# Expert units: second products behind their own first products, another product order, other buffer counts

## The chip, the cores and the metric

The kernel runs as one program on one core of a Trainium2 chip. The metric is the device time of one execution in microseconds (us). Engines are named as in the profile: PE (TensorE, matmuls; PEld are its weight loads), DVE (VectorE), ACT (ScalarE), POOL (GpSimd) and SP (SyncE, which issues the DMAs of weights). PSUM is the memory that matmuls write to, in banks of 128x512 float32; SBUF holds all else.

## The reference, cut to what matters

```python
x = attention(q, k, v, proj)            # 2 x 768 tokens, 8 heads of 64, bucket mask
x = rational_ffn(x, w_in, w_out, a, b)  # h = x @ w_in; g = P(h) / Q(h); x = g @ w_out
# experts: N = 1536 tokens, D = 512, E = 8, F = 1024
P = exp(x @ w_gate - max)
for _ in range(8):                      # Sinkhorn: rows, then columns
    P /= P.sum(1, keepdims=True) + 1e-9
    P /= P.sum(0, keepdims=True) + 1e-9
    P *= N / E
out = 0
for e in range(E):
    out += P[:, e:e+1] * (relu(x @ w1[e]) @ w2[e])
```

All of it is float32. The kernel splits each operand into a high and a low part in a rounded type (`fp32r`) and sums three products, high x high, high x low and low x high.

## The kernel before, in words

The program has three stages: attention (to about 287 us of the profiled execution), the dense layer (to 578 us) and the experts (to the end). The change touches the end of the dense layer and the experts.

**Units.** The expert stage works on 64 units. Unit u is a quarter q of an expert's hidden columns (256 of them; q runs over 8 experts x 4) and a batch b of 768 tokens, u = 2q + b. With 256 hidden columns, 512 inputs and 768 tokens the first layer is a product of 2x2 blocks, done with seven products in place of eight (`unit_b`, L546). Product m multiplies a sum of weight blocks (`ww`, a tile for two of them, built by POOL in `w_blocks`, L497) by a sum of token blocks (`xb`, built once for each batch in `x_blocks`, L463). One product is six matmuls of 384 columns into one of four PSUM banks (`product`, L529).

**From a product to a hidden block.** ACT copies product 1 to `m1`; DVE adds the others to running sums `u2` and `u3`, and four times writes a hidden block `c` (L559). ACT rounds relu(c) to `gh` (L554), and DVE computes the low part `gl` from `c` and `gh` (L555), both of them in SBUF. A pair (gh, gl) is for a half f of the hidden columns and a half g of the tokens.

**Second products.** `second_b(u, t)` (L588), t = 0 to 5, multiplies 128 tokens of a token half g = t // 3 by the expert's second weights `wb` (split by POOL in `w_second`, L518): six matmuls of 512 columns into one of three PSUM banks, hidden half f = 0 first, then 1. DVE adds the bank to `osum`, times the gate's weight (L610; L608 while expert 0 runs, and ACT copies for q = 0).

**Order.** The stage is recorded by hand, step by step, and each engine executes its own instructions in that order. Before, the main loop (L883) puts one second product of unit u - 1 behind each first product of unit u but the first, and steps of the gate between them. `ORDER` (L427) is the order of the products. POOL's blocks for q + 1 are recorded step by step along the units of q, into five weight tiles used in turn (L494), so POOL has to wait until PE is done with a tile. `w_second(q)` is recorded in the first step of unit 2q.

**Gate.** `gate_steps` (L624) computes logits (`lp`, 40 matmuls), transposes them (`lt`), then the maximum and eight Sinkhorn iterations, in which PE sums columns (`cp`) and DVE does the rest. It uses a single PSUM bank of its own (`sum_bank(3, ..)`).

Of the kernel before, what the change touches and what calls it, by code (L numbers as in the profile page):

```python
# [15 lines left out]
F32R = mybir.dt.float32r  # L16
# [19 lines left out]
def kernel(  # L36
# [18 lines left out]
    B, H, S, D = q.shape  # L55
# [368 lines left out]

    ORDER = (1, 6, 7, 4, 2, 5, 3)  # L427
    xb, wb_, ww = {}, {}, {}

    def tokens(half, b, g, a, z):  # L430
# [32 lines left out]
    def x_blocks(b):  # L463

        x_given(b, 1, 0, 0, pool_lo)
        if b == 0:
            x_given(b, 2, 1, 0, pool_lo)
        yield
        t1 = x_temp("t1")
        for a, z in pieces(b, 0, 1):  # L470
            dve.tensor_tensor(t1[:, :, a:z], tokens(0, b, 1, a, z), tokens(0, b, 0, a, z), ALU.subtract)
        t2 = x_temp("t2")
        for a, z in pieces(b, 1):
            dve.tensor_tensor(t2[:, :, a:z], tokens(1, b, 1, a, z), t1[:, :, a:z], ALU.subtract)
        yield
        x_sum(b, 6, t2, dve_lo)
        x_sum(b, 5, t1, pool_lo)
        yield
        t3 = x_temp("t3")
        for a, z in pieces(b, 1):  # L480
            dve.tensor_tensor(t3[:, :, a:z], tokens(1, b, 1, a, z), tokens(0, b, 1, a, z), ALU.subtract)
        x_sum(b, 7, t3, pool_lo)
        yield
        for a, z in pieces(b, 0):
            dve.tensor_tensor(t2[:, :, a:z], tokens(1, b, 0, a, z), t2[:, :, a:z], ALU.subtract)
        x_sum(b, 4, t2, dve_lo)
        yield
        if b:
            x_given(b, 2, 1, 0, pool_lo)
        x_given(b, 3, 1, 1, pool_lo)  # L490

    def w_pair(q, k):

        r = (q * 4 + k) % 5  # L494
        return wslots[0].tile([P, 2, 2, 2, P], F32R, tag=("wa0", "wa1", "wa2", "wa3", "wb0")[r], name="ww")

    def w_blocks(q, stemp):  # L497

# [19 lines left out]
    def w_second(q):  # L518

        r = raws[1, CB + q]  # L520
        for f in range(2):
            k = (2 * q + f) % 4
            t = (wslots[0] if k < 3 else late).tile([P, 2, 512], F32R, tag=f"wb{k + 1}" if k < 3 else "w", bufs=1,
                                                    name="wb")
            split(pool_hi, pool_lo, t[:, 0], t[:, 1], r[:, f])
            wb_[q, f] = t
        load_weights(1, CB + q + 2)

    def product(o, q, b, m):  # L529
        w, x = ww[q, m], xb[b, m]  # L530
# [6 lines left out]
    bhid = {}  # L537

    def hidden_b(u, f, g):
        bhid[u, f, g] = tuple(late.tile([P, GC], F32R, tag=t, bufs=8, name=t) for t in ("gh", "gl"))  # L540
        return bhid[u, f, g]

    def temp_b(name, bufs=1):
# [2 lines left out]
    def unit_b(u):  # L546

        q, b = divmod(u, B)
        m1, u2, u3 = temp_b("m1"), temp_b("u2"), temp_b("u3")
        low = []  # L550

        def high(f, g, c):
            gh, gl = hidden_b(u, f, g)
            act.activation(gh, c, AF.Relu)  # L554
            low.append(lambda: dve.scalar_tensor_tensor(gl, c, 0.0, gh.bitcast(F32), ALU.max, ALU.subtract))  # L555

        def add(x, o, f, g):
            c = temp_b("c", 3)
            dve.tensor_tensor(c, o, x, ALU.add)  # L559
            high(f, g, c)  # L560

        def prod(m):
            o = hidden_bank(next(turn) % 4, "prod")[:, 0:GC]
            product(o, q, b, m)
            return o

        act_copy(m1, prod(1))
        yield
        dve.tensor_tensor(u2, prod(6), m1, ALU.add)
        yield  # L570
        dve.tensor_tensor(u3, prod(7), u2, ALU.add)  # L571
        yield
        add(u3, prod(4), 1, 0)
        yield
        low.pop()()
        add(m1, prod(2), 0, 0)
        yield
        low.pop()()
        p5 = prod(5)
        add(u3, p5, 1, 1)  # L580
        dve.tensor_tensor(u2, p5, u2, ALU.add)
        yield
        low.pop()()
        add(u2, prod(3), 0, 1)
        yield
        low.pop()()

    def second_b(u, t):  # L588

        q, b = divmod(u, B)  # L590
        e, p = divmod(q, FP)
        g, i = divmod(t, 3)
        o = sum_bank(0, "accb")
        ts = slice(i * P, (i + 1) * P)
        for f in range(2):
            gh, gl = bhid[u, f, g]
            w = wb_[q, f]
            for m, (l, r) in enumerate(((gh, w[:, 0]), (gh, w[:, 1]), (gl, w[:, 0]))):
                pe.matmul(o, lhsT=l[:, ts], rhs=r, start=f == 0 and m == 0, stop=f == 1 and m == 2)  # L599
        n = b * 6 + t  # L600
        if q == 0 and t % 2 == 0:
            k = n // 2
            osum[k] = sums.tile([P, 2, 512], F32, tag=f"sum{k // 2}{k % 2}", name="osum")
        d = osum[n // 2][:, t % 2]
        if q == 0:
# [18 lines left out]
    def gate_steps():  # L624

        gp = const.tile([P, NT, E], F32, name="gp")
        for b in range(B):
            for g in range(2):

                blocks = ((1, 0), (2, 1)) if g == 0 else ((1, 0), (5, 0), (3, 1))  # L630
                lp = sum_bank(3, "lp")
                ops = [(w, xb[b, m][:, j, c], 2 * half + c) for m, half in blocks for c in range(2)
                       for w, j in ((wg2, 0), (wg2, 1))]
                for n, (w, x, c) in enumerate(ops):
                    pe.matmul(lp[0:2 * E, 0:GC], lhsT=w[:, c], rhs=x, start=n == 0, stop=n == len(ops) - 1)
                yield
                ls = temp_b("ls")[0:2 * E]
                act_copy(ls, lp[0:2 * E, 0:GC])
                yield
                lt = sum_bank(3, "lt")  # L640
                for j in range(3):
                    pe.transpose(lt[:, 2 * j * E:2 * (j + 1) * E], ls[:, j * P:(j + 1) * P], idf[0:2 * E, 0:2 * E])
                n = b * 6 + g * 3
                yield
                dve.tensor_reduce(gp[:, n:n + 3, :], lt[:, 0:6 * E].rearrange("p (t k e) -> p t e k", k=2, e=E),
                                  AX.X, ALU.add)
        m1 = const.tile([P, 2], F32, name="gm")
        dve.tensor_reduce(m1[:, 0:1], gp, AX.XY, ALU.max)
        ones = temp_b("ls")[:, 0:P]
# [10 lines left out]
        yield  # L660
        dve.tensor_scalar(m1[:, 1:2], mb[:, 0:1], -1.0, None, ALU.mult)
        act.activation(gp, gp, AF.Exp, bias=m1[:, 1:2])
        yield
        rsum = const.tile([P, NT], F32, name="rsum")
        csum = const.tile([P, E], F32, name="csum")
        for _ in range(8):
# [1 line left out]
            dve.tensor_scalar(rsum, rsum, 1e-9, None, ALU.add)  # L668
            dve.reciprocal(rsum, rsum)
            dve.tensor_tensor(gp, gp, rsum.unsqueeze(2).broadcast_to((P, NT, E)), ALU.mult)  # L670
            yield
            yield
            cp = sum_bank(3, "cp")
            pe.matmul(cp[:, 0:NT * E], lhsT=ones, rhs=gp.rearrange("p t e -> p (t e)"), start=True, stop=True)
# [132 lines left out]
    with tc.manual_schedule(engines={mybir.EngineType.PE, mybir.EngineType.Activation, mybir.EngineType.DVE,  # L807
# [3 lines left out]
        for s in range(NS + QF):  # L811
# [41 lines left out]
                go(xgen)  # L853
            acting = [new] if n < 0 else []

            if s == NS - QS + ALAG + 3:
                def stemp():
                    c = [conv.tile([P, 512], F32, tag="c", name="c").rearrange("p (k c f) -> p k c f", k=2, c=2)
                         for _ in range(2)]
                    return c[0][:, 0], c[0][:, 1], c[1][:, 0]  # L860
                ws = w_blocks(0, stemp)
            if ws is not None and s < NS:
                go(ws)
            if n == 0:
                x_stack.close()
                xs[0] = ffn_pool("x0", 1)
# [10 lines left out]
        def stemp():  # L877
            t = x_temp("st").rearrange("p c (f k) -> p (c f k)", k=P).rearrange("p (k c f) -> p k c f", k=3, c=2)
            return t[:, 0], t[:, 1], t[:, 2]

        gating = gate_steps()
        SECOND = {1: 0, 2: 1, 3: 2, 4: 3, 5: 4, 6: 5}
        for u in range(NB_ + 1):  # L883
            q, b = divmod(u, B)
            first = unit_b(u) if u < NB_ else None
            for k in range(len(ORDER)):
                if first:
                    go(first)
                if u and k in SECOND:
                    second_b(u - 1, SECOND[k])  # L890
                if u >= 1:
                    go(gating)
                if u == 0:
                    if k == 0:
                        xgen = x_blocks(1)
                    go(xgen)
                if u < NB_:
                    if b == 0 and k == 0:
                        w_second(q)
                        ws = w_blocks(q + 1, stemp) if q + 1 < E * FP else None  # L900
                    if ws is not None and (b == 1 and k < 4 or b == 0 and 2 <= k < 5):
                        go(ws)
            if first:
                go(first)
            if u in (FP * B, FP * B + 1):
                weight_b(u - FP * B)


# [28 lines left out]
```

## Time and profile before

| | |
|---|---|
| median of 3 runs | 1613.9 us (1613.78 to 1615.29) |
| the profiled execution | 1613.6 us, span 1611.8 us |
| PE busy | 1549.2 us (96%), 8071 matmuls |
| DVE / POOL / ACT busy | 1224.9 / 930.0 / 621.0 us |
| mean granted TensorE clock | 0.994 |

The span runs from the first to the last instruction; 1.8 us lie around it. Matmuls are pipelined: a matmul's own duration (337 ns for 384 columns) is longer than the distance from its start to the next one's start, so PE's pace is read from starts and not from durations. "Idle before" gives what an engine waited for just before a group of instructions.

### The profile page before, as it was taken

What the parts mean: (1) busy time and instruction counts of PE and PEld (TensorE: products, weight loads), DVE (VectorE), ACT (ScalarE), POOL (GpSimd) and SP (SyncE); (2) the same over time, 40 slices, a digit from 0 to 9 for tenths busy, and PEclk for the clock granted to TensorE, in tenths of its full rate; (3) what the DMA queues carried; (4) which work ended last, traced back from release to release, by engine and by line L of the source; (5) the groups of instructions that cost most, each with busy time, mean ns of one, the idle gap of its engine ahead of it and who ended that gap; (6) DMA issues with size and microseconds to landing.
All of it is one profiled execution on the core that took longest, in us unless ns stands there. A gap on an engine that the chain in (4) does not pass through costs nothing.

```text
span 1611.8 us, 22139 instructions
## 1 busy us (share of the span) xinstructions
PE 1549.2 (96%) x8071; PEld 1354.4 (84%) x8071; DVE 1224.9 (76%) x2116; ACT 621.0 (39%) x1167; POOL 930.0 (58%) x1165
## 2 busy tenths in 40 slices
PE   5989999899999979999999999999999999999999
PEld 4888888777666868898989899898989989898987
DVE  7989989788999983786667767666766766676675
ACT  4888788787767833111111111111111111111111
POOL 7788785677777874456455345445534544553450
PEclk9999999999999989999999999999999999999999
DMA  5323220011111000011011001101100110110002
GB/s 168 86 81 90 69 76 15 27 53 61 57 53 66 1 26 27 27 40 40 27 34 45 27 27 40 40 27 38 42 27 27 40 40 27 39 40 27 27 1 78
DMA packets 49404, 71.83 MB, mean 45 GB/s; under 512 B 4368, under 2 KB 35088, under 8 KB 49296
## 3 DMA queue, kind: packets, MB, share of 16 engines
q1 hardware_dynamic: 48432, 68.85, 13.8%
q8 instruction: 64, 1.05, 0.3%
q10 hardware_dynamic: 864, 1.57, 0.3%
q14 instruction: 44, 0.36, 0.1%
HBM read 59.79 MB, written 3.15 MB: 39 GB/s over the span
## 4 chain that ended last, share of the span: by engine, by line
PE 71%; DVE 16%; ACT 5%; POOL 4%; issue 4%; DMA 1%; SPq 0%; POOLq 0%; DVEq 0%
PE accb L599 33%; PE prod L534 28%; PE av L323 2%; PE pt L308 2%; DVE tq L382 2%; DVE tu L384 2%; DVE tr L383 2%; POOL e L294 2%; PE acca L405 2%; PE h L354 1%; DVE e L285 1%; DVE bits L182 1%; DVE bits L180 1%; DVE tu L376 1%; DVE ptl L109 1%
## 5 line engine op out<-in xcount | busy, mean ns | idle before, releaser
L534 PE MATMUL prod<-xb,ww 128*128 128x384 f32 x2688 | 534.2, 337 | 5.7 <-DVE u L571 2.4
L534 PEld LDWEIGHTS prod<-xb,ww 128*128 128x128 f32 x2688 | 479.9, 189 | 40.7 <-ACT xb L106 2.9
L599 PE MATMUL accb<-wb,gh 128*128 128x512 f32 x1536 | 478.8, 393 | 0.0
L554 ACT ACTIVATE gh<-c 128x384 fp32r<-128x384 f32 x256 | 134.6, 526 | 764.5 <-DVE c L559 764.5
L610 DVE SCALAR_TENSOR_TENSOR osum<-accb,gp,osum 128x512 f32<-128x512 f32 x336 | 251.9, 750 | 208.3 <-PE accb L599 206.2
L599 PEld LDWEIGHTS accb<-wb,gh 128*128 128x128 f32 x1536 | 283.9, 188 | 36.4
L599 PE MATMUL accb<-wb,gl 128*128 128x512 f32 x768 | 305.9, 398 | 4.2 <-DVE gl L555 4.2
L100 POOL TENSOR_SCALAR ww<-ra 128x256 fp32r<-128x256 f32 x128 | 52.4, 410 | 407.9 <-PE prod L534 407.6
L555 DVE SCALAR_TENSOR_TENSOR gl<-c,gh 128x384 fp32r<-128x384 f32 x256 | 199.4, 779 | 4.5 <-ACT gh L554 4.3
L599 PEld LDWEIGHTS accb<-wb,gl 128*128 128x128 f32 x768 | 144.4, 188 | 35.1 <-DVE gl L555 4.6
L354 PE MATMUL h<-xh,wa 128*128 128x512 f32 x384 | 127.5, 395 | 5.8 <-DVE tu L377 5.6
L405 PE MATMUL acca<-gh,wb 128*128 128x512 f32 x384 | 128.0, 394 | 4.9 <-DVE part L417 2.6
L559 DVE TENSOR_TENSOR c<-prod,u 128x384 f32<-128x384 f32 x192 | 106.1, 552 | 27.2 <-PE prod L534 27.0
L109 DVE TENSOR_TENSOR ptl<-pt,pth 128x512 fp32r<-128x512 f32 x144 | 94.4, 681 | 19.0 <-ACT pth L106 18.2
L103 POOL TENSOR_TENSOR ww<-ra,ww 128x256 fp32r<-128x256 f32 x128 | 94.8, 740 | 10.7
L294 POOL TENSOR_SCALAR e<-e,rs 128x768 f32<-128x768 f32 x96 | 88.7, 934 | 19.6 <-DVE rs L292 10.1
L354 PEld LDWEIGHTS h<-xh,wa 128*128 128x128 f32 x384 | 72.1, 188 | 27.1 <-DVE tu L377 10.0
L405 PEld LDWEIGHTS acca<-gh,wb 128*128 128x128 f32 x384 | 72.1, 188 | 25.7 <-ACT gh L106 5.1
L285 DVE TENSOR_SCALAR_CACHE_REDUCE e<-s 128x768 f32<-128x768 f32 x96 | 90.8, 947 | 1.3 <-PE s L278 0.9
L308 PE MATMUL pt<-idr,e 128*128 128x128 f32 x576 | 81.3, 275 | 11.0 <-POOL e L294 4.7
L286 ACT ACTIVATE e<-e,nm 128x768 f32<-128x768 f32 x96 | 89.8, 935 | 3.5 <-DVE e L285 2.8
L103 POOL TENSOR_TENSOR wb<-rb,wb 128x512 fp32r<-128x512 f32 x64 | 84.3, 1317 | 5.3
(168 smaller groups left out, 2429.9 us busy)
## 6 DMA issues: line engine op xcount, KB each, us to landing
ra<-in_moe_w_dram SPq DMA_DIRECT2D x32, 512.0 KB
rb<-in_moe_w_dram SPq DMA_DIRECT2D x32, 512.0 KB
ra<-in_moe_w_in_dram SPq DMA_DIRECT2D x16, 512.0 KB
rb<-in_moe_w_out_dram SPq DMA_DIRECT2D x16, 512.0 KB
qkv<-in_q_dram SPq DMA_DIRECT2D x16, 192.0 KB
qkv<-in_k_dram SPq DMA_DIRECT2D x16, 192.0 KB
qkv<-in_v_dram SPq DMA_DIRECT2D x16, 192.0 KB
a<-a SPq DMA_DIRECT2D x16, 192.0 KB
```

Of the source, the lines that this page charges most:

```text
L103: pool.tensor_tensor(lo, src, hi.bitcast(F32), ALU.subtract)
L109: dve.tensor_tensor(lo, src, hi.bitcast(F32), ALU.subtract)
L285: dve.tensor_scalar(e[j], s[:, 0:S], BIG, None, ALU.min, ALU.min, accum_out=nm)
L294: pool.tensor_scalar(e[j], e[j], rs[:, j:j + 1], 0.0, ALU.mult, ALU.add)
L308: pe.transpose(pt[:, c, j * P:(j + 1) * P], e[j][:, cc * P:(cc + 1) * P], idf)
L354: pe.matmul(hps, lhsT=a[:, c], rhs=x[:, c], start=m == 0, stop=m == 3 * KC - 1)
L405: pe.matmul(o, lhsT=l[:, js], rhs=r, start=f == 0 and m == 0, stop=f == QF - 1 and m == 2)
L534: pe.matmul(o, lhsT=w[:, i, c], rhs=x[:, j, c], start=n == 0, stop=n == 5)
L554: act.activation(gh, c, AF.Relu)
L555: low.append(lambda: dve.scalar_tensor_tensor(gl, c, 0.0, gh.bitcast(F32), ALU.max, ALU.subtract))
L599: pe.matmul(o, lhsT=l[:, ts], rhs=r, start=f == 0 and m == 0, stop=f == 1 and m == 2)
L610: dve.scalar_tensor_tensor(d, o, gate["p"][:, n, e:e + 1], d, ALU.mult, ALU.add)
```

## The change

Each unit now does its seven products in a row and then its own six second products in a row. The order of the products is 1, 2, 6, 7, 4, 5, 3. Second products of the second token half take hidden half 1 first. The pairs (gh, gl) have four buffers where they had eight, and weight tiles are eight where they were five; `w_blocks(q + 1)` and `w_second(q + 1)` are both recorded along the units of q. At the end of the dense layer, `w_blocks(0)` starts two steps earlier and `w_second(0)` follows it. The gate's steps stand at other places, and `weight_b`, which multiplies expert 0's sums by the gate, stands ahead of the unit's products.

```diff
-    ORDER = (1, 6, 7, 4, 2, 5, 3)
+    ORDER = (1, 2, 6, 7, 4, 5, 3)
...
         x_given(b, 1, 0, 0, pool_lo)
-        if b == 0:
-            x_given(b, 2, 1, 0, pool_lo)
+        x_given(b, 2, 1, 0, pool_lo)
...
-        r = (q * 4 + k) % 5
+        r = (q * 4 + k) % 8
...
-        load_weights(1, CB + q + 2)
+            if f:
+                load_weights(1, CB + q + 2)
+            yield
...
-        bhid[u, f, g] = tuple(late.tile([P, GC], F32R, tag=t, bufs=8, name=t) for t in ("gh", "gl"))
+        bhid[u, f, g] = tuple(late.tile([P, GC], F32R, tag=t, bufs=4, name=t) for t in ("gh", "gl"))
         act_copy(m1, prod(1))
         yield
+        add(m1, prod(2), 0, 0)
+        yield
         dve.tensor_tensor(u2, prod(6), m1, ALU.add)
+        low.pop()()
         yield
         dve.tensor_tensor(u3, prod(7), u2, ALU.add)
         yield
         add(u3, prod(4), 1, 0)
         yield
-        low.pop()()
-        add(m1, prod(2), 0, 0)
-        yield
-        low.pop()()
         p5 = prod(5)
         add(u3, p5, 1, 1)
+        low.pop(0)()
         dve.tensor_tensor(u2, p5, u2, ALU.add)
         yield
-        low.pop()()
         add(u2, prod(3), 0, 1)
+        low.pop(0)()
         yield
         low.pop()()
...
-        for f in range(2):
+        for n, f in enumerate((g, 1 - g)):
...
-            if s == NS - QS + ALAG + 3:
+            if s == NS - QS + ALAG + 1:
...
-            if ws is not None and s < NS:
-                go(ws)
+            if ws is not None and s < NS and not go(ws):
+                if s == NS - 2:
+                    wsec = w_second(0)
+                go(wsec)
...
+        GATE = {0: ((), range(6)), 1: (range(4), range(1, 6)), 2: (range(4), (2, 3))}
+        xgen = x_blocks(1)
+        for u in range(NB_):
             q, b = divmod(u, B)
+            if b == 0:
+                wsec = ws = iter(())
+                if q + 1 < E * FP:
+                    wsec, ws = w_second(q + 1), w_blocks(q + 1, stemp)
+            if u in (FP * B, FP * B + 1):
+                weight_b(u - FP * B)
+            first = unit_b(u)
+            gk, gt = GATE.get(u, ((0, 1), (2, 3)))
             for k in range(len(ORDER)):
+                go(first)
+                if k in gk:
+                    go(gating)
+                if u == 0 and k == 1:
+                    go(xgen)
+                if b == 0 and k in (2, 4):
+                    go(wsec)
+                if b == 1 and k in (0, 2, 4):
+                    go(ws)
+            for t in range(6):
+                second_b(u, t)
+                if t == 0:
                     go(first)
+                if t in gt:
                     go(gating)
+                if u == 0 and t < 5:
+                    go(xgen)
+                if u and (b == 0 and t in (0, 3) or b == 1 and t in (0, 3)) or u == 1 and t in (4, 5):
+                    go(ws)
```

On PE, in a unit of the middle of the expert stage, before (`prod` is a first product, `accb` a second one):

```order
L534 MATMUL prod<-xb,ww 128x384 x12
L599 MATMUL accb<-wb,gh 128x512 x2
L599 MATMUL accb<-wb,gl 128x512
L599 MATMUL accb<-wb,gh 128x512 x2
L599 MATMUL accb<-wb,gl 128x512
L534 MATMUL prod<-xb,ww 128x384 x6
```

And with the change, the last second product of one unit, the products of the next, and its first second product:

```order
L599 MATMUL accb<-wb,gh 128x512 x2
L599 MATMUL accb<-wb,gl 128x512
L534 MATMUL prod<-xb,ww 128x384 x42
L599 MATMUL accb<-wb,gh 128x512 x2
L599 MATMUL accb<-wb,gl 128x512
```

Where six groups of six alternated with the products, a unit now has one run of 42 matmuls of 384 columns and one of 36 of 512.

On DVE, in a unit of the middle with the change (L571 is u2's first sum, L574 is u3's, L581 adds product 5 to u2, L610 adds a second product to `osum`):

```order
L559 TENSOR_TENSOR c<-prod,m_11072 128x384
L571 TENSOR_TENSOR u_11073<-prod,m_11072 128x384
L555 SCALAR_TENSOR_TENSOR gl<-c,gh 128x384
L574 TENSOR_TENSOR u_11074<-prod,u_11073 128x384
L559 TENSOR_TENSOR c<-prod,u_11074 128x384 x2
L555 SCALAR_TENSOR_TENSOR gl<-c,gh 128x384
L581 TENSOR_TENSOR u_11073<-prod,u_11073 128x384
L559 TENSOR_TENSOR c<-prod,u_11073 128x384
L555 SCALAR_TENSOR_TENSOR gl<-c,gh 128x384
L610 SCALAR_TENSOR_TENSOR osum<-accb,gp,osum 128x512
L555 SCALAR_TENSOR_TENSOR gl<-c,gh 128x384
```

The sums of the second products stood between the first ones' sums; now all but the last `gl` stand ahead of them, and the second `gl` is one that the unit's own first second product reads.

On DVE at the start of the expert stage, before (the sums `u` and `c` of unit 0, with L471, L474 and L481, which make the token blocks of batch 1, between them):

```order
L569 TENSOR_TENSOR u_6800<-prod,m_6799 128x384
L471 TENSOR_TENSOR t_6831<-part 128x2x256
L471 TENSOR_TENSOR t_6831<-part 128x2x128
L474 TENSOR_TENSOR t_6834<-part,t_6831 128x768
L571 TENSOR_TENSOR u_6801<-prod,u_6800 128x384
L109 TENSOR_TENSOR xb<-t_6834,xb 128x768
L559 TENSOR_TENSOR c<-prod,u_6801 128x384
L481 TENSOR_TENSOR t_6868<-part 128x768
L555 SCALAR_TENSOR_TENSOR gl<-c,gh 128x384
```

And with the change (L470, L473 and L480 are the same lines; L645 reads the gate's first transposed logits out of its only bank):

```order
L559 TENSOR_TENSOR c<-prod,u_6808 128x384
L555 SCALAR_TENSOR_TENSOR gl<-c,gh 128x384 x2
L470 TENSOR_TENSOR t_6924<-part 128x2x256
L470 TENSOR_TENSOR t_6924<-part 128x2x128
L473 TENSOR_TENSOR t_6927<-part,t_6924 128x768
L109 TENSOR_TENSOR xb<-t_6927,xb 128x768
L480 TENSOR_TENSOR t_6958<-part 128x768
L645 TENSOR_REDUCE gp<-lt 128x24
```

Batch 1's blocks now come behind all sums of unit 0, and the gate's L645 comes behind most of those blocks.

## Rows read from the trace of the kernel before

**Rows 1.** The page's first section: busy time, share and instructions of each engine.

```profile
PE 1549.2 (96%) x8071; PEld 1354.4 (84%) x8071; DVE 1224.9 (76%) x2116; ACT 621.0 (39%) x1167; POOL 930.0 (58%) x1165
```

**Rows 2.** Busy time by stretches: length, engines (instructions), granted clock, DMA share, GB/s.

```profile
550.00:566.00 16.00, 16.00 (x72) 13.25 (x72) 15.09 (x23) 12.75 (x21) 13.99 (x16) 1.00 0.02 5
...
577.90:588.40 10.50, 7.20 (x37) 6.06 (x35) 9.48 (x11) 3.52 (x8) 7.96 (x6) 1.00 0.00 0
588.40:595.20 6.80, 6.11 (x18) 4.55 (x19) 3.18 (x4) 1.83 (x3) 6.55 (x7) 0.50 0.21 69
595.20:602.00 6.80, 2.34 (x12) 1.44 (x9) 5.89 (x6) 2.21 (x3) 6.63 (x7) 1.00 0.02 8
602.00:608.90 6.90, 5.50 (x15) 4.75 (x16) 5.31 (x9) 3.71 (x8) 6.19 (x6) 0.51 0.00 0
708.39:1584.23 875.84, 875.84 (x4369) 787.79 (x4369) 607.88 (x956) 145.61 (x281) 435.45 (x621) 1.00 0.10 32
```

**Rows 3.** The chain that ended last, dense layer, units 7 and 63: start, length.

```profile
556.32 2.72 PE h L354 x12
...
708.39 2.08 PE prod L534 x12
...
1584.23 2.08 PE prod L534 x12
```

**Rows 4.** PE's instructions in time order, one unit: start, length, what.

```profile
1271.27 2.25 PE L534 MATMUL prod<-xb,ww 128*128 128x384 f32 x12
1273.35 0.63 PE L599 MATMUL accb<-wb,gh 128*128 128x512 f32 x2
...
1283.08 0.63 PE L599 MATMUL accb<-wb,gh 128*128 128x512 f32 x2
...
1284.47 1.21 PE L534 MATMUL prod<-xb,ww 128*128 128x384 f32 x6
1285.52 0.63 PE L599 MATMUL accb<-wb,gh 128*128 128x512 f32 x2
```

**Rows 5.** PE's last 42 matmuls, all of 512 columns.

```profile
1598.32 0.63 PE L599 MATMUL accb<-wb,gh 128*128 128x512 f32 x2
...
1606.52 0.62 PE L599 MATMUL accb<-wb,gh 128*128 128x512 f32 x2
```

**Rows 6.** All engines in time order, unit 0: ACT's first copy, DVE's token blocks.

```profile
582.63 0.47 ACT L106 ACTIVATE m<-prod 128x384 f32<-128x384 f32 x1
...
583.87 2.83 DVE L471 TENSOR_TENSOR t<-part 128x512 f32<-128x512 f32 x2
...
589.01 1.75 DVE L109 TENSOR_TENSOR xb<-t,xb 128x768 fp32r<-128x768 f32 x1 [0.44 <-ACT xb L106]
...
594.41 1.47 DVE L481 TENSOR_TENSOR t<-part 128x768 f32<-128x768 f32 x1 [3.18 <-POOL xb L103]
...
597.27 3.20 DVE L485 TENSOR_TENSOR t<-part,t 128x512 f32<-128x512 f32 x2
```

**Rows 7.** The page's groups: busy, mean ns of one, idle before and its releaser.

```profile
L100 POOL TENSOR_SCALAR ww<-ra 128x256 fp32r<-128x256 f32 x128 | 52.4, 410 | 407.9 <-PE prod L534 407.6
...
L559 DVE TENSOR_TENSOR c<-prod,u 128x384 f32<-128x384 f32 x192 | 106.1, 552 | 27.2 <-PE prod L534 27.0
```

**Rows 8.** DVE and POOL in time order: `gl` alone and beside POOL.

```profile
1126.51 0.55 DVE L555 SCALAR_TENSOR_TENSOR gl<-c,gh 128x384 fp32r<-128x384 f32 x1
...
1128.91 1.30 POOL L103 TENSOR_TENSOR wb<-rb,wb 128x512 fp32r<-128x512 f32 x1
1128.94 1.68 DVE L555 SCALAR_TENSOR_TENSOR gl<-c,gh 128x384 fp32r<-128x384 f32 x1
```

**Rows 9.** DVE in time order: the sum behind a second product.

```profile
1284.67 0.75 DVE L610 SCALAR_TENSOR_TENSOR osum<-accb,gp,osum 128x512 f32<-128x512 f32 x1 [0.28 <-PE accb L599]
```

**Rows 10.** DVE in time order: a Sinkhorn iteration's first step, and what follows its eighth.

```profile
659.84 0.25 DVE L676 TENSOR_REDUCE csum<-cp 128x8 f32<-128x96 f32 x1
...
662.91 1.09 DVE L555 SCALAR_TENSOR_TENSOR gl<-c,gh 128x384 fp32r<-128x384 f32 x1
```

More of the change, by code (lines that the diff above doesn't have):

```diff
@@ L487, in x_blocks @@
         yield
-        if b:
-            x_given(b, 2, 1, 0, pool_lo)
         x_given(b, 3, 1, 1, pool_lo)
     def w_pair(q, k):
-        r = (q * 4 + k) % 5
-        return wslots[0].tile([P, 2, 2, 2, P], F32R, tag=("wa0", "wa1", "wa2", "wa3", "wb0")[r], name="ww")
+        r = (q * 4 + k) % 8
+        return (wslots[0] if r < 5 else late).tile([P, 2, 2, 2, P], F32R, bufs=1, name="ww",
+                                                   tag=("wa0", "wa1", "wa2", "wa3", "wb0", "w5", "w6", "w7")[r])
     def w_blocks(q, stemp):
@@ L598, in second_b @@
             for m, (l, r) in enumerate(((gh, w[:, 0]), (gh, w[:, 1]), (gl, w[:, 0]))):
-                pe.matmul(o, lhsT=l[:, ts], rhs=r, start=f == 0 and m == 0, stop=f == 1 and m == 2)
+                pe.matmul(o, lhsT=l[:, ts], rhs=r, start=n == 0 and m == 0, stop=n == 1 and m == 2)
         n = b * 6 + t
@@ L646, in gate_steps @@
                                   AX.X, ALU.add)
+                yield
         m1 = const.tile([P, 2], F32, name="gm")
@@ L662, in gate_steps @@
         act.activation(gp, gp, AF.Exp, bias=m1[:, 1:2])
-        yield
         rsum = const.tile([P, NT], F32, name="rsum")
@@ L670, in gate_steps @@
             dve.tensor_tensor(gp, gp, rsum.unsqueeze(2).broadcast_to((P, NT, E)), ALU.mult)
-            yield
             yield
@@ L879, in stemp @@
             return t[:, 0], t[:, 1], t[:, 2]
+        assert not go(wsec)
         gating = gate_steps()
-        SECOND = {1: 0, 2: 1, 3: 2, 4: 3, 5: 4, 6: 5}
-        for u in range(NB_ + 1):
+        GATE = {0: ((), range(6)), 1: (range(4), range(1, 6)), 2: (range(4), (2, 3))}
+        xgen = x_blocks(1)
+        for u in range(NB_):
             q, b = divmod(u, B)
-            first = unit_b(u) if u < NB_ else None
-            for k in range(len(ORDER)):
-                if first:
+            if b == 0:
[3 more added lines that the diff above has]
+            if u in (FP * B, FP * B + 1):
+                assert "p" in gate
+                weight_b(u - FP * B)
+            first = unit_b(u)
+            gk, gt = GATE.get(u, ((0, 1), (2, 3)))
+            for k in range(len(ORDER)):
+                go(first)
[10 more added lines that the diff above has]
+                if t == 0:
@@ L888 @@
                     go(first)
-                if u and k in SECOND:
-                    second_b(u - 1, SECOND[k])
-                if u >= 1:
+                if t in gt:
                     go(gating)
-                if u == 0:
-                    if k == 0:
-                        xgen = x_blocks(1)
+                if u == 0 and t < 5:
                     go(xgen)
[L897 to L906, printed above, removed]
+                if u and (b == 0 and t in (0, 3) or b == 1 and t in (0, 3)) or u == 1 and t in (4, 5):
+                    go(ws)
+            if b:
+                go(wsec), go(ws)
+                assert not go(ws)
 _INS = ['q', 'k', 'v', 'proj', 'moe_w_in', 'moe_w_out', 'moe_a', 'moe_b', 'moe2_w_gate', 'moe2_w1', 'moe2_w2']
```

## The prediction

> **What bounds the kernel now.** I read the busy times first: PE has 96% [rows 1], so what can be won lies in PE's idle time or in its pace. The stretches come next. From 708.39 to 1584.23 us PE is busy in every microsecond at a granted clock of 1.00, while DVE has 608 and POOL 435 of those 876 us [rows 2]. The chain's last two rows are the first products of units 7 and 63; 56 units in 875.84 us make 15.64 us each, and units in between start on the same grid [rows 3]. So here only PE's pace counts. The place with idle PE is the start of the expert stage, 577.9 to 608.9 us: PE idles there for 3.30 + 0.69 + 4.46 + 1.40 = 9.85 us, and in two stretches its clock is 0.50 and 0.51, the lower of its two levels (1.2 of 2.4 GHz) [rows 2].
>
> **PE's pace.** Distances between starts say what a group costs. In a unit, twelve products' matmuls take 2.08 us (1271.27 to 1273.35), a lone six 1.05 (1284.47 to 1285.52), six second ones 1.39 (1283.08 to 1284.47) [rows 4]. With five lone sixes and six groups of second ones: 2.08 + 5 x 1.045 + 6 x 1.39 = 15.64. The kernel's end has 42 matmuls of 512 columns in a row. There 36 from the start of the run take 8.20 us (1598.32 to 1606.52) [rows 5]. In the dense layer, where every matmul has 512 columns, twelve take 2.72, that is 1.36 for six [rows 3], and six times that is 8.16. So a group of 512 columns that follows 384 columns costs some 0.03 us more than its like in a long run, and a long run pays that about once, not at each group. The change makes one run of 36 out of six groups: 8.20 for 8.34. Its 42 products at the pace of the twelve take 3.5 x 2.08 = 7.28 for 7.30. A unit comes to 15.48; with the rows' last digits the gain is 0.14 to 0.17, I take 0.155. There are 63 such units, since the first products of unit 0 and the second ones of unit 63 stood alone before: **-9.8 us**, if nothing new waits.
>
> A rule speaks against this term: the Trainium skill, "TensorE: Matmul & The Clock Gate", section "Wait — 56ns, not 53.3ns?", gives a matmul's start-to-start distance as its columns at 2.4 GHz and about 2.5 ns, whatever stands before it. By it the order would not matter and the term would be 0. The rows differ: six equal matmuls take 1.39 or 1.36 us by where they stand [rows 3, 4].
>
> **Does the new order let PE wait inside a unit?** I put the rows' durations into DVE's new order, time 0 at the first product, 1.04 us a product, and 0.2 for a hand-over (DVE's sum starts at 1284.67, 0.20 behind the start of the group after the one it reads [rows 4, 9]). A `c` takes 0.55 [rows 7], `gl` 0.55 alone and 1.68 beside a POOL operation of 1.30 [rows 8]. Product 2 ends at 2.1, `c` at 2.8; product 6's sum at 3.9, the first `gl` at 4.4, u3 at 5.0, product 4's `c` at 5.9, product 5's at 7.0, the second `gl` at 7.5. The first second product begins at 7.28 and reads that `gl` with its sixth matmul, at 8.4: 0.9 spare. The other two are read from the fourth second product on, at 11.9 and 12.6, and end at about 9.2 and 10.5. The sums need 6 x 0.75 [rows 9] in 8.2 us, so PSUM banks come back in time.
>
> POOL is different in units of batch 0. Before, it waited 408 us for PE to leave a weight tile [rows 7]. With eight tiles it only waits for `wb`, which PE leaves at the end of a unit of batch 1, and then does all 22 operations for q + 1 in one burst. The two `gl` then meet POOL. The first meets a 1.30 operation and ends at about 4.8; u3 at 5.3, the two `c` as before, since they read PSUM and wait for the products. The second meets at worst another 1.30: 7.0 + 1.68 = 8.7, a wait of 0.3; but only two of the 22 are that long, both early, and by then it meets the shorter ones, whose `gl` lie near 0.83 to 1.2, so it ends at 7.8 to 8.2. I take no wait; bounds 0 to 0.3 for each of 32 units, 0 to 9.6 us.
>
> **The start of the expert stage.** Lost before: 9.85 idle and half of 6.11 + 5.50 at the lower clock, 5.8 [rows 2], together 15.7. With the change:
> - POOL's `w_second(0)` moves into the dense layer's last steps, ahead of its last `gl`; token blocks come up to 1.5 us later, I take 1.0. Product 4 is now the fifth and needs product 1's bank, which ACT's copy of m1 frees, and that still comes behind batch 0's blocks: at 583.1 before [rows 6], now 584.1. PE is there at 577.9 + 4 x 1.04 = 582.1: 2.0.
> - Unit 0's second products find their `gl` done. But the gate's second logits need the gate's only bank, and DVE frees it behind batch 1's blocks: sums of unit 0 end near 591.3, then 2.83 (L470's pair), 1.4 (L473, half of that), a wait of about 1 for ACT, 1.75, 1.47 [rows 6] = 599.8. PE has done its products at 587.3, five second products (6.9) and the gate's eight (1.4) at 595.8: 4.0.
> - The next transposes need ACT's copy behind its last two block copies, which wait for L484 (3.20, [rows 6]): near 606.3, PE at 604.4: 1.9.
> - PE is then as idle as from 595.2 to 602.0, where 2.34 busy us of 6.80 came ahead of the clock 0.51 [rows 2]. A like fall costs up to 3.4; part lies beside the wait before: 1.0.
> Sum 8.9 for 15.7: **-6.8**, bounds -11 (no such waits beyond the first) to +1 (each block twice as late).
>
> **The gate in units 3 to 6.** An iteration's eight DVE operations took 3.07 us (659.84 to 662.91 [rows 10]). One now stands behind product 2's `c`, ahead of all sums that PE's next run needs, and pushes the second `gl` from 7.5 to 8.6 at least, to 10 where POOL is in its burst: 0.3 in two units and 1.7 in two, 4.0 at worst; I take **+2.0**. The dense layer's earlier POOL work (2.6 us at its first step) lies in steps in which POOL had room; +0.2.
>
> Sum: -9.8 - 6.8 + 2.0 + 0.2 = -14.4 on the profiled execution's 1613.6; the median shown is 1613.9, so 1599.5.
>
> **The rivals.**
> - **A, the pace stays** (columns alone set it, and the end of the kernel ran faster because DVE and POOL were nearly idle there). For it: a long run behind products is seen once. Against it: the dense layer has the faster pace [rows 3] while DVE, ACT and POOL are busy for 15.1, 12.8 and 14.0 of 16 us [rows 2]. Then 9.8 less is gained: 1609.3. The rule of the Trainium skill above would give the same.
> - **B, the start gains nothing**: batch 1's blocks, behind unit 0's sums, hold the gate's bank and unit 1's products for as long as before. For it: all of these are longer beside POOL [rows 6]. Then -9.8 + 2 + 0.2: 1606.3.
> - **C, slower**: the second `gl` holds PE in every unit of batch 0 because POOL's burst stretches both `gl` and the sums behind them come late enough to hold PSUM banks as well. The price is the wait times 32; from 0.45 us a unit on it eats all 14.4. If both meet a 1.30 operation each time, 0.4 for `gl` and as much for the banks, 0.8 x 32 = 25.6: 1625. Against it: only two of 22 operations are so long.
> - **D, it does not do what it says** has no room: the order of PE's rows shows the runs.
>
> **How the numbers follow.** Forecast 0.72 (its own range 1593 to 1605), A 0.07, B 0.13, C 0.08. A measurement of this kernel tells 0.2%, 3.2 us, from no change. The forecast, A and most of B lie below 1610.7; a twentieth between A and C lies within: faster 0.89, same 0.04, slower 0.07. The range 1590 to 1609 leaves out C, part of A and a tenth of the forecast.
>
> **What would show it.** In the profile after: products' rows of 42 at 7.28 us and units 15.48 apart in the middle; an excess of the first two groups alone in each run of second products; one wait of about 4 us of PE ahead of the second logits and less than 10 us lost up to unit 1; `gl` of 0.8 to 1.7 in units of batch 0 and 0.55 in those of batch 1, POOL idle in much of the latter. Units of batch 0 that are longer than those of batch 1 would show C, units 15.64 apart A.

## The result, and the profile after

The changed kernel takes 1599.9 us (median of 5 runs, 1599.12 to 1600.68) against 1613.9 (5 runs): a ratio of 0.9909, 95% interval 0.9896 to 0.9923. Its profiled execution spans 1597.5 us where the one before spans 1611.8, 14.3 us less; the forecast was 14.4 less.

The page's busy times, beside [rows 1]: every engine executes as many instructions as before, PE in 7.2 us less, and PE's share is now 97%.

```profile
PE 1542.0 (97%) x8071; PEld 1353.8 (85%) x8071; DVE 1198.4 (75%) x2116; ACT 621.0 (39%) x1167; POOL 940.2 (59%) x1165
```

The chain that ended last, units 7, 8 and 63 (start, length, what), which answers to [rows 3]: a unit is one piece of 42 products and one of 36 second ones.

```profile
709.86 7.30 PE prod L534 x42
717.17 8.20 PE accb L599 x36
725.37 7.30 PE prod L534 x42
...
1578.23 7.30 PE prod L534 x42
```

56 units in 1578.23 - 709.86 = 868.37 us make 15.507 each, for 15.64. The stretches, which answer to [rows 2]: the first four are unit 0 from its first product on and the units behind it, the last one the 56 units.

```profile
579.31:588.56 9.25, 7.60 (x43) 7.28 (x42) 8.11 (x13) 5.17 (x11) 5.53 (x4) 1.00 0.00 0
588.56:600.72 12.16, 9.10 (x43) 6.30 (x42) 10.78 (x13) 5.08 (x10) 10.46 (x9) 1.00 0.13 43
600.72:604.13 3.41, 3.41 (x11) 1.54 (x12) 2.33 (x3) 3.13 (x5) 2.03 (x2) 0.50 0.02 5
604.13:621.00 16.87, 16.87 (x88) 14.13 (x87) 6.31 (x14) 5.72 (x11) 13.23 (x19) 1.00 0.10 31
709.86:1578.23 868.37, 868.37 (x4370) 787.43 (x4369) 581.39 (x953) 145.31 (x280) 434.51 (x606) 1.00 0.10 33
```

PE idles 1.65 + 3.06 = 4.7 us here where it idled 9.85 in [rows 2], and one stretch of 3.41 us has the lower clock where two longer ones had. The two waits, in time order: product 4 waits for ACT to free product 1's bank, the gate's second logits for DVE to free the gate's bank, as forecast.

```profile
584.78 0.47 ACT L106 ACTIVATE m<-prod 128x384 f32<-128x384 f32 x1
585.31 3.41 PE L534 MATMUL prod<-xb,ww 128*128 128x384 f32 x18 [1.65 <-ACT m L106]
...
600.46 0.20 DVE L645 TENSOR_REDUCE gp<-lt 128x24 f32<-128x48 f32 x1
...
600.71 1.78 PE L635 MATMUL lp<-xb,wg 128*16 128x384 f32 x5 [3.06 <-DVE gp L645]
```

Two of the page's groups, the first of which answers to [rows 7]: POOL's waits have moved from PE's products to the second weights `wb`, and all 256 `gl` together waited 1.1 us.

```profile
L100 POOL TENSOR_SCALAR wb<-rb 128x512 fp32r<-128x512 f32 x64 | 40.2, 628 | 409.4 <-PE accb L599 409.4
...
L555 DVE SCALAR_TENSOR_TENSOR gl<-c,gh 128x384 fp32r<-128x384 f32 x256 | 164.3, 642 | 1.1 <-ACT gh L554 0.7
```

In time order, a unit of batch 0 from 1252.43 us and one of batch 1 from 1267.94: the first two `gl` of each, and the beginning of POOL's burst.

```profile
1252.43 7.47 PE L534 MATMUL prod<-xb,ww 128*128 128x384 f32 x42
1252.69 0.62 POOL L100 TENSOR_SCALAR wb<-rb 128x512 fp32r<-128x512 f32 x1 [14.21 <-PE accb L599]
...
1255.36 1.30 POOL L103 TENSOR_TENSOR wb<-rb,wb 128x512 fp32r<-128x512 f32 x1
1256.25 0.82 DVE L555 SCALAR_TENSOR_TENSOR gl<-c,gh 128x384 fp32r<-128x384 f32 x1
...
1259.37 0.71 DVE L555 SCALAR_TENSOR_TENSOR gl<-c,gh 128x384 fp32r<-128x384 f32 x1
...
1267.94 7.47 PE L534 MATMUL prod<-xb,ww 128*128 128x384 f32 x42
...
1271.76 0.55 DVE L555 SCALAR_TENSOR_TENSOR gl<-c,gh 128x384 fp32r<-128x384 f32 x1
...
1274.88 0.55 DVE L555 SCALAR_TENSOR_TENSOR gl<-c,gh 128x384 fp32r<-128x384 f32 x1
```

The second `gl` ends 7.65 us behind the first product in batch 0 and 7.49 in batch 1; the sixth second matmul, which reads it, starts at 8.46. The two units are equally long.

### The profile page after: what moved, and what is told of

It is laid out like the page before. It is cut to its first block, busy times and chain, and to the rows that moved or that the text cites. A ratio compares the mean times of both kernels' runs of the same rounds, so it can differ in the third digit from the quotient of the medians.

```text
span 1597.5 us, 22272 instructions
## 1 busy us (share of the span) xinstructions
PE 1542.0 (97%) x8071; PEld 1353.8 (85%) x8071; DVE 1198.4 (75%) x2116; ACT 621.0 (39%) x1167; POOL 940.2 (59%) x1165
## 3 DMA queue, kind: packets, MB, share of 16 engines
HBM read 59.79 MB, written 3.15 MB: 39 GB/s over the span
## 4 chain that ended last, share of the span: by engine, by line
PE 70%; DVE 15%; ACT 5%; POOL 4%; issue 3%; DMA 0%; SPq 0%; DVEq 0%; POOLq 0%; ACTq 0%
PE accb L599 32%; PE prod L534 28%; PE av L323 2%; PE pt L308 2%; DVE tq L382 2%; DVE tu L384 2%; DVE tr L383 2%; PE acca L405 2%; POOL e L294 1%; PE h L354 1%; DVE bits L182 1%; DVE bits L180 1%; DVE e L285 1%; DVE tu L376 1%; DVE ptl L109 1%
## 5 line engine op out<-in xcount | busy, mean ns | idle before, releaser
L534 PE MATMUL prod<-xb,ww 128*128 128x384 f32 x2688 | 480.5, 335 | 2.1 <-ACT m L106 1.6
L534 PEld LDWEIGHTS prod<-xb,ww 128*128 128x128 f32 x2688 | 469.0, 188 | 8.0 <-ACT m L106 2.0
L610 DVE SCALAR_TENSOR_TENSOR osum<-accb,gp,osum 128x512 f32<-128x512 f32 x336 | 251.7, 749 | 127.9 <-PE accb L599 126.2
L599 PE MATMUL accb<-wb,gl 128*128 128x512 f32 x768 | 300.4, 391 | 0.4 <-DVE gl L555 0.4
L100 POOL TENSOR_SCALAR wb<-rb 128x512 fp32r<-128x512 f32 x64 | 40.2, 628 | 409.4 <-PE accb L599 409.4
L106 ACT ACTIVATE m<-prod 128x384 f32<-128x384 f32 x64 | 31.5, 492 | 452.5 <-PE prod L534 452.4
L555 DVE SCALAR_TENSOR_TENSOR gl<-c,gh 128x384 fp32r<-128x384 f32 x256 | 164.3, 642 | 1.1 <-ACT gh L554 0.7
L559 DVE TENSOR_TENSOR c<-prod,m 128x384 f32<-128x384 f32 x64 | 35.7, 558 | 92.5 <-PE prod L534 92.5
```

The lines of the kernel that those rows point to most:

```text
L534: pe.matmul(o, lhsT=w[:, i, c], rhs=x[:, j, c], start=n == 0, stop=n == 5)
L599: pe.matmul(o, lhsT=l[:, ts], rhs=r, start=n == 0 and m == 0, stop=n == 1 and m == 2)
```

## Where the 14.3 us are

From the starts of the units' first products in the trace, us from one unit to the next (before, a unit's second products lie in the next unit, so unit 0 is short there; the rows below "after" are eight experiments of the next section, each from one profiled execution):

| kernel | unit 0 | 1 | 2 | 3 | 4 | 5 | 6 | 7 | middle |
|---|---|---|---|---|---|---|---|---|---|
| before | 13.46 | 32.16 | 18.75 | 16.75 | 16.79 | 16.24 | 16.16 | 15.64 | 15.64 |
| after | 26.43 | 20.50 | 16.43 | 16.03 | 17.49 | 16.03 | 17.47 | 15.51 | 15.51 |
| pairs | 13.46 | 34.18 | 18.68 | 19.68 | 18.07 | 16.27 | 16.18 | 15.64 | 15.64 |
| threes | 13.43 | 35.78 | 19.72 | 18.05 | 17.70 | 16.19 | 18.45 | 15.57 | 15.57 |
| gate_late | 20.35 | 23.38 | 16.13 | 16.44 | 17.50 | 16.03 | 17.49 | 15.76 | 15.51 |
| sink | 27.58 | 20.52 | 16.40 | 16.01 | 17.69 | 16.01 | 17.69 | 15.51 | 15.51 |
| five | 26.36 | 20.51 | 16.40 | 17.31 | 17.17 | 17.28 | 17.15 | 15.51 | 15.51 |
| old_order | 26.23 | 21.26 | 16.39 | 16.57 | 18.89 | 16.57 | 20.48 | 15.50 | 15.50 |
| calm | 26.29 | 20.51 | 16.40 | 16.03 | 15.78 | 16.03 | 15.78 | 16.24 | 15.51 |
| calm_late | 20.42 | 23.35 | 16.71 | 16.64 | 15.78 | 16.03 | 15.78 | 16.24 | 15.51 |

What a row has above its own pace is the loss; it holds PE's own matmuls for the gate as well as its waits. Units 0 to 2 before: 64.37, less 7.30 and two units of 15.64, leaves 25.79; after 63.36 less three of 15.507 leaves 16.84. Units 3 to 6: 65.94 - 62.56 = 3.38 before, 67.02 - 62.03 = 4.99 after. So:

| | forecast | measured |
|---|---|---|
| pace, 63 units | -9.8 | 63 x 0.133 = -8.4 |
| start, units 0 to 2 | -6.8 | -8.9 |
| gate, units 3 to 6 | +2.0 | +1.6 |
| ahead of unit 0 | +0.2 | +1.4 |
| sum | -14.4 | -14.3 |

## The experiments

Ratios are against the kernel before, which was timed beside each of three groups of experiments (its medians were 1614.5, 1615.3 and 1614.6 us). The changed kernel was not timed again beside them, so what an edit is worth against it rests on the units' starts above more than on medians 1 or 2 us apart. `pairs` and `threes` are edits of the kernel before, the others of the changed one.

**pairs, threes: is it the length of the runs?** The kernel before, with its second products in three runs of twelve, or two of eighteen; nothing else changes.

```diff
-        SECOND = {1: 0, 2: 1, 3: 2, 4: 3, 5: 4, 6: 5}
+        SECOND = {2: (0, 1), 4: (2, 3), 6: (4, 5)}     # pairs
+        SECOND = {3: (0, 1, 2), 6: (3, 4, 5)}          # threes
...
-                if u and k in SECOND:
-                    second_b(u - 1, SECOND[k])
+                for t in SECOND.get(k, ()) if u else ():
+                    second_b(u - 1, t)
```

> The kernel before, with two second products behind every second first product (runs of 12 matmuls of 512 columns, three a unit, in place of six runs of 6). Theory (a run of 512 columns pays about 0.04 us once, whatever its length): units in the middle start 15.58 us apart (36 x 0.2267 + 3 x 0.041 + products 7.30) for 15.64; 63 units make -3.8 us, and the start may gain a few us more, since unit 0's first second product comes later in unit 1. Rival (columns alone set the pace, long runs were only seen where other engines were quiet): 15.64 as before.

> The kernel before, with three second products behind the fourth and the seventh first product (runs of 18, two a unit). Theory: units 15.54 us apart (36 x 0.2267 + 2 x 0.041 + 7.30), 63 units make -6.3 us, and the start as in the runs of 12. Rival (columns alone): 15.64.

Measured: pairs 1620.9 us, 1.0042 (1.0027 to 1.0057), middle units 15.64; threes 1620.19, 1.0035 (1.0022 to 1.0049), middle units 15.57. Both lose at the start (units 0 to 6 take 6.2 and 9.0 us more; each has one wait of PE of 5.6 us for ACT's `gh`, where before has one of 4.2 for a `gl`). In the middle, threes gained 0.07 us a unit of the 0.10 expected and pairs nothing of its 0.06. Both expectations failed, and PE's rows in time order say why. Pairs:

```profile
1257.42 2.27 PE L534 MATMUL prod<-xb,ww 128*128 128x384 f32 x12
1259.53 0.63 PE L599 MATMUL accb<-wb,gh 128*128 128x512 f32 x2
...
1262.29 3.31 PE L534 MATMUL prod<-xb,ww 128*128 128x384 f32 x18
1265.44 0.63 PE L599 MATMUL accb<-wb,gh 128*128 128x512 f32 x2
...
1268.20 2.27 PE L534 MATMUL prod<-xb,ww 128*128 128x384 f32 x12
```

And threes:

```profile
1257.05 3.31 PE L534 MATMUL prod<-xb,ww 128*128 128x384 f32 x18
1260.19 0.63 PE L599 MATMUL accb<-wb,gh 128*128 128x512 f32 x2
...
1264.32 4.35 PE L534 MATMUL prod<-xb,ww 128*128 128x384 f32 x24
1268.50 0.63 PE L599 MATMUL accb<-wb,gh 128*128 128x512 f32 x2
```

Twelve products take 2.11 (1257.42 to 1259.53) and eighteen 3.15 behind a run of twelve second ones; behind a run of six, twelve took 2.08 [rows 4]. So a long run of 512 columns makes the first products behind it slower too. Single starts in the trace give both sides. At rest a product matmul takes 173.3 ns and a second one 226.7. The first nine of a run of second ones take 41 ns more in all (29 where the run is only six); the first six products take 26 more behind twelve or more second matmuls, and 4 behind six. A unit at rest is 42 x 173.3 + 36 x 226.7 = 15.44 us; each long run adds 0.067 and each short one 0.033. Six short make 15.64, three long 15.64, two long 15.57, one 15.51: the four middles that were measured. Pairs is slow by arithmetic: half as many switches at twice the price.

**late_gl: how much room has the second `gl`?** It goes behind `u2`'s sum and product 3's `c`.

```diff
         add(u3, p5, 1, 1)
-        low.pop(0)()
         dve.tensor_tensor(u2, p5, u2, ALU.add)
         yield
         add(u2, prod(3), 0, 1)
+        low.pop(0)()
         low.pop(0)()
```

> The changed kernel with the second low part gl computed behind product 3's sum in place of ahead of product 5's, so it ends about 1.0 us later. Theory (PE reads it 8.45 us into a unit, and it ends at 7.5 us with POOL idle and 7.65 beside POOL): it would end at 8.55 in units of batch 1 and 8.7 to 9.3 in units of batch 0, so PE waits about 0.15 and 0.3 to 0.9; 64 units make 14 to 34 us, 1614 to 1634. Rival (DVE's order has spare time enough, as in the kernel before): 1600.

Measured: 1628.62 us, 1.0087 (1.0072 to 1.0102); middle units 15.83 in batch 1 and 16.09 in batch 0. This `gl` ends at 8.61 and 8.87 us. PE's weight loads wait for `gl` 55 times (the view of waits, 720 to 1600 us: total, times, longest):

```profile
PEld accb L599 <- DVE gl L555: 32.9, 55, 0.7
```

So rival C's mechanism exists, and the seam is narrow: 1.1 to 1.2 us later costs 0.32 and 0.58 us a unit. Both fit a deadline of 8.29 us, which leaves the changed kernel 0.80 us in batch 1 and 0.64 in batch 0. Only the place of that one instruction keeps the changed kernel clear of it.

**five: are eight weight tiles needed?**

```diff
-        r = (q * 4 + k) % 8
+        r = (q * 4 + k) % 5
```

> The changed kernel with five weight tiles in place of eight, nothing else. Theory (the gain is from the order and the start, and POOL has time enough to fill five tiles between PE's uses, in units of batch 1): 1599.9 within 1.5 us, units of the middle 15.51 apart, POOL waiting for PE's products again. Rival (POOL running ahead is what the change lives on): units of batch 0 wait for weights at their first products, 1605 or more.

Measured: 1602.22 us, 0.9924 (0.9907 to 0.9941). The middle stays 15.51, though POOL again waits for PE's products (its groups from 580 to 1600 us):

```profile
L100 POOL TENSOR_SCALAR ww<-st 128x256 fp32r<-128x256 f32 x93 | 58.4, 628 | 276.3 <-PE prod L534 273.6
```

Units 3 to 6 take 68.91 us for 67.02: the three more tiles are worth 1.9 us, in the gate's units alone. I had expected none of it, and the median is 2.3 us above the changed kernel's where at most 1.5 was expected.

**gate_late: the gate's bank at the start.** Unit 0 runs two gate steps fewer, so that the second logits come behind unit 1's products.

```diff
-        GATE = {0: ((), range(6)), 1: ...
+        GATE = {0: ((), range(4)), 1: ...
```

> The changed kernel with the gate's second logits recorded in unit 1 (behind its first product) in place of unit 0 (behind its fifth second product), two gate steps later; nothing else. Theory (PE's 3.2 us wait there is for the gate's only bank, which DVE frees behind batch 1's token blocks, and the fall of the clock behind it comes from that wait): the wait goes, the clock stays at 1.00, and up to 1 us comes back as a wait for ACT's copy: -2 to -4.5 us, about 1596.5. Rival (PE would wait for batch 1's blocks in unit 1 instead): 1599 to 1600.

Measured: 1596.92 us, 0.9884 (0.9871 to 0.9898); units 0 to 7 take 143.09 for 145.90. The wait of 3.06 and the lower clock (half of 3.41) are gone, together 4.8, and two shorter waits come (1.2 for ACT's logits, 0.6 for an `osum`). The stretch that was slow now has PE busy throughout at a granted clock of 1.00:

```profile
600.00:604.00 4.00, 4.00 (x25) 2.97 (x24) 2.92 (x5) 3.03 (x5) 1.96 (x2) 1.00 0.13 48
```

**sink: the Sinkhorn steps out of the products.** All of an iteration's steps move behind the second products.

```diff
-            gk, gt = GATE.get(u, ((0, 1), (2, 3)))
+            gk, gt = GATE.get(u, ((), (0, 1, 4, 5)))
```

> The changed kernel with the Sinkhorn steps of units 3 to 6 behind second products 0, 1, 4 and 5 in place of products 1 and 2 and second products 2 and 3; nothing else. Theory (units 4 and 6 are 17.5 us long and units 3 and 5 16.0, because DVE's eight small operations, slowed by POOL's burst, stand ahead of the sums that PE's next run reads): units 4 and 6 fall to 16.0 to 16.2, -2 to -2.9 us, about 1597.5. Rival (the time is PE's own, for the gate's matmuls): no change.

Measured: 1599.37 us, 0.9896 (0.9880 to 0.9911): no gain, the expectation failed. The four executions lie between 1597.39 and 1600.19 us, so this rests on units 4 and 6, which take 17.69 us for 17.48. In the changed kernel the eight DVE operations stand between `c` and `u2` of units 4 and 6, and L676 and others are stretched beside POOL (chain, start and length):

```profile
661.32 0.56 DVE c L559
...
662.07 0.87 DVE csum L676
...
665.00 0.47 DVE u L571
...
667.80 0.92 DVE gl L555
...
668.76 3.24 PE accb L599 x13
```

In sink they stand behind the previous unit's last second products, and there they meet the next unit's burst; DVE and two of POOL's operations in time order:

```profile
659.86 0.25 DVE L675 TENSOR_REDUCE csum<-cp 128x8 f32<-128x96 f32 x1
660.02 1.30 POOL L103 TENSOR_TENSOR wb<-rb,wb 128x512 fp32r<-128x512 f32 x1
660.15 1.20 DVE L676 TENSOR_SCALAR csum<-csum 128x8 f32<-128x8 f32 x1
...
661.38 0.20 DVE L677 RECIPROCAL csum<-csum 128x8 f32<-128x8 f32 x1
...
661.99 1.29 POOL L103 TENSOR_TENSOR wb<-rb,wb 128x512 fp32r<-128x512 f32 x1
662.04 0.25 DVE L667 TENSOR_REDUCE rsum<-gp 128x12 f32<-128x96 f32 x1
662.33 0.98 DVE L668 TENSOR_SCALAR rsum<-rsum 128x12 f32<-128x12 f32 x1
...
664.02 0.54 DVE L559 TENSOR_TENSOR c<-prod,m 128x384 f32<-128x384 f32 x1
```

The eight take 4.2 us (659.86 to 664.02) for 3.07 [rows 10] and 3.1 in unit 4 of the changed kernel (alone, from 656.76 us on there, 2.04), and the unit's first `c` starts 5.0 us behind the unit's first product, where it starts 2.6 behind it in the changed kernel. The edit only moved the collision.

**both: gate_late and sink together.**

> The two edits together, gate's second logits two steps later and the Sinkhorn steps behind second products 0, 1, 4, 5. If they act at separate places: the sum of both, -4 to -7 us, about 1594.5. If the two extra steps push the Sinkhorn work into unit 7 with a new wait there, less.

Measured: 1597.19 us, 0.9888 (0.9874 to 0.9901); units 4 and 6 take 17.68. The sum of both, about 1594.5, did not come: all of the gain is gate_late's.

**calm: the steps only where POOL is quiet.** Units of batch 0 (2, 4, 6, ...) get no gate step among their products; those of batch 1 keep both.

```diff
-            gk, gt = GATE.get(u, ((0, 1), (2, 3)))
+            gk, gt = GATE.get(u, ((0, 1) if b else (), (2, 3)))
```

> The changed kernel with no Sinkhorn step behind a first product in units of batch 0 (units 4 and 6), where POOL's burst runs; the steps go on into unit 7. Theory (units 4 and 6 are 17.5 us because DVE's eight operations alternate with POOL's burst ahead of the sums that PE's next run reads; behind second products 4 and 5 they had met the burst's longest operations, so that edit gained nothing): units 4 and 6 fall to 15.8, unit 7 rises to 16.0, -2.5 to -3 us, about 1597. Rival (the gate costs PE's own time, wherever it stands): no change.

Measured: 1596.39 us, 0.9888 (0.9873 to 0.9903). Units 4 and 6, now with one iteration each for two, take 15.78 for 17.48; the steps that they no longer do run on into unit 7, which takes 16.24. The iteration's place, not its length, cost PE the time.

**calm_late: both cures.** Calm and gate_late together, with two more steps in unit 2.

```diff
-        GATE = {0: ((), range(6)), 1: (range(4), range(1, 6)), 2: (range(4), (2, 3))}
+        GATE = {0: ((), range(4)), 1: (range(4), range(1, 6)), 2: (range(4), range(1, 5))}
...
-            gk, gt = GATE.get(u, ((0, 1), (2, 3)))
+            gk, gt = GATE.get(u, ((0, 1) if b else (), (2, 3)))
```

> The same with the gate's second logits in unit 1 as well, and two more gate steps behind unit 2's second products to make up for it. If the waits are separate: both gains, -5 to -6 us to 1594.5. If unit 2's four steps in a row make PE wait, up to 2 us less.

Measured: 1593.74 us, 0.9874 (0.9858 to 0.9891), the fastest of all. What PE still waits for from 575 to 760 us (total, times, longest):

```profile
PE prod L534 <- ACT m L106: 1.6, 1, 1.6
PE lt L642 <- ACT ls L106: 1.2, 1, 1.2
PE accb L599 <- ACT osum L106: 0.6, 1, 0.6
PE cp L673 <- DVE gp L670: 0.4, 1, 0.4
```

**old_order, old_calm: what is the product order worth?** The new rows with the old order of products; old_calm has calm's edit as well.

```diff
-    ORDER = (1, 2, 6, 7, 4, 5, 3)
+    ORDER = (1, 6, 7, 4, 2, 5, 3)
...
         act_copy(m1, prod(1))
         yield
-        add(m1, prod(2), 0, 0)
-        yield
         dve.tensor_tensor(u2, prod(6), m1, ALU.add)
-        low.pop()()
         yield
...
         add(u3, prod(4), 1, 0)
         yield
+        add(m1, prod(2), 0, 0)
+        low.pop(0)()
+        yield
```

> The changed kernel with the products in the old order 1, 6, 7, 4, 2, 5, 3 (the sums and low parts follow), rows of seven and six as in the change. Theory (the new order brings both pairs of the first second product early): the low part that the third matmul of the first second product reads ends near 7.5 us in units of batch 1, with 0.2 us spare, and up to 0.5 late beside POOL in units of batch 0; at the start PE waits for product 4's block one product earlier, +1.8: in all +2 to +14, about 1605. Rival (the order of the products does not matter): 1600.

> Rows of seven and six in the old product order, with no Sinkhorn step behind a first product in units of batch 0. Theory (the old order cost 4.4 us only in units 3 to 6, where a late DVE met PE, since units of the middle are 15.50 apart in either order): the cost goes in units 4 and 6 and 0.5 us each stays in units 3, 5 and 7, 1598 to 1599.5. Rival (the old order costs its time at the start, in unit 0's blocks): 1601 or more.

Measured: old_order 1604.27 us, 0.9919 (0.9906 to 0.9932); old_calm 1600.10, 0.9909 (0.9894 to 0.9923). The middle is 15.50, so the order costs nothing there, where I had expected up to 0.5 a unit in batch 0. At the start it costs nothing either: unit 0 takes 26.23 for 26.43, since PE waits 1.7 us in all for batch 0's blocks but not the 1.6 for ACT's first copy. Units 3 to 6 take 72.51 us for 67.02; PE waits there 3.6 us for `gl`, and in unit 6 the clock falls once more. So the time came near the 1605 expected, but by another path. Two of the five executions took 1599.91 and 1600.12 us at a mean granted clock of 0.998, the other three 1604.27 to 1604.43 at 0.992 or 0.993, the profiled one among them; what the order costs where the clock holds is in no trace here. Old_calm ended just above the 1598 to 1599.5 expected. Its units 4 and 6 are cured (15.75 and 15.80), while 3, 5, 7, 8 and 9 take 0.5 to 0.9 more than calm's (16.57, 16.57, 16.89, 16.43, 16.10). So the order matters only where a gate step makes DVE late.

## Why the prediction was right, by its steps

**Pace: the mechanism held, its size was off by 1.4 us.** A run of 36 second matmuls takes 8.20, as forecast. The 42 matmuls of the products take 7.31 and not 7.28: that step took the pace of twelve behind a run of six [rows 4]. Pairs and threes measured the price of a switch back from a long run (26 ns for 4), but the trace of before held it once: in unit 0, behind the dense layer's run of 512 columns, the first six products take 1.066 us from start to start (577.918 to 578.984), where a lone six takes 1.044. Rival A is refuted: from 720 to 1560 us POOL is busy for 421 us before, 424 in pairs and 416 in threes, DVE for 582, 568 and 556, so the other engines work nearly as before, and the runs set the four paces. The rule of the Trainium skill ("TensorE: Matmul & The Clock Gate", section "Wait — 56ns, not 53.3ns?") would give an equal spacing in all four kernels; the trace has 15.64, 15.64, 15.57 and 15.51 us a unit. Its 215.7 ns for 512 columns also lies below the 226.7 measured here at rest, and the measurement decides.

**No wait inside a unit: right.** From 720 to 1600 us PE waited for nothing. In batch 0 the second `gl` ended at 7.65 (7.8 to 8.2 forecast), in batch 1 at 7.49 (7.5). Late_gl shows that the margin was real and small, 0.6 to 0.8 us for the 0.9 worked out.

**Start: right in place, -8.9 for -6.8.** Product 4 waited 1.65 us (2.0 forecast), the second logits 3.06 (4.0), the lower clock cost 1.7 (1.0). (The prediction's own terms give 4.2 for the second of these, since 587.3 + 6.9 + 1.4 is 595.6 and not 595.8; and its bound of -11, "no such waits beyond the first", does not follow, since 15.7 less 2.0 is 13.7.) The wait of 1.9 ahead of the transposes is missing: from 604.13 to 621.00 PE waits for nothing. ACT's copy came as late as forecast (606.89 for 606.3), and the transposes' weight load still waited for it, but PE had hardly arrived:

```profile
606.43 0.46 ACT L106 ACTIVATE ls<-lp 16x384 f32<-16x384 f32 x1
...
606.94 0.26 PEld L642 LDWEIGHTS lt<-idr,ls 16*128 16x128 f32 x3 [0.31 <-ACT ls L106]
```

PE ran at half its clock just ahead of that and so came 1.7 us later; I had added two terms that lie beside each other. That the one covers the other is a reading of these rows and no run separates them: in gate_late, where the clock holds, the transposes wait 1.2 us, but the logits stand elsewhere too. The losses sum to 6.4 for 8.9, which is about the difference. Rival B is refuted by the 8.9 us that the start gained.

**Gate: +1.6 for +2.0, at its place.** The eight operations in a unit of batch 0 cost about 1.5 us each in units 4 and 6, those in batch 1 nothing; calm takes it away. The second `gl` ended at 8.40 us in units 3 and 5 and at 10.0 in 4 and 6, for the 8.6 and 10 worked out. The sum was partly luck: the prices of 0.3 and 1.7 a unit make 4.0, of which the prediction took half without a reason. PE lost 2.9 us to waits here, and 1.3 already in these units before, for which the prediction had no term (an iteration's own matmuls, 0.26 us, are taken off in both).

**Ahead of unit 0: +1.4 for +0.2, most of it not the change's.** The dense layer itself takes 0.24 us more, as forecast. Its first matmul starts 1.1 us later (288.8 for 287.7), in code that is the same. The first 40 us of the span, before:

```profile
0.00:40.00 40.00, 22.04 (x120) 17.48 (x121) 29.40 (x76) 17.67 (x36) 28.43 (x38) 0.91 0.56 169
```

And after:

```profile
0.00:40.00 40.00, 24.33 (x116) 19.60 (x117) 29.61 (x75) 17.25 (x35) 28.42 (x38) 0.83 0.59 169
```

The clock was lower for longer there. Over the thirteen kernels that start moved between 287.7 and 291.8 us, whatever the edit. So the total came out closer (0.1 us) than its terms did (up to 2.1): the errors cancelled.

**Open:** why the first matmuls behind a change of the column count are slower. No run took types, weights and columns apart, and the length of the runs is not all: in old_order, whose runs are as long as the change's, the first nine second matmuls take 30 ns more and not 41. Nor was it tried to shorten the wait of 1.6 for ACT's first copy, which every version with the new order keeps. The four buffers for the pairs, the other order of the hidden halves and POOL's earlier work in the dense layer were not taken apart from the rest, so what each of them gives to the start is not shown.

## What to carry to other kernels

Where one engine is busy throughout, read its pace from starts and compare the same group in different neighbourhoods: a different order of the same work was worth 0.13 us of a unit's 15.64 here, with no wait removed. Price a switch in both directions and at several run lengths before gathering work, since fewer, longer runs can cost as much as many short ones. A side job on a shared engine is moved to where its neighbours are quiet, not merely later: sink and calm moved the same operations, and only one of them gained.

## What the runs showed that was not expected

- The price of a switch depends on the run before it: products behind six second matmuls lose 4 ns in all, behind twelve or more 26.
- Beside POOL, it depends on the operation what a small one on DVE pays: in sink, L676 (TENSOR_SCALAR, 128x8 elements) took 1.20 us beside a POOL operation of 1.30 and L668 (128x12) 0.98, each 0.17 alone. L667 (TENSOR_REDUCE) and L677 (RECIPROCAL) have their data in SBUF too, ran wholly beside POOL operations, and kept their 0.25 and 0.20.
- Eight weight tiles for five took 274 us of POOL's waits for PE's products away, and gave PE 1.9 us.
